# Blockwise causal attention and a gated unit on one core: q and k loaded nine tokens to a partition, two pairs on the two halves, under a new written order

## The chip, the core and the metric

The kernel runs on one NeuronCore of a Trainium2 chip. TensorE (PE in the profile, its weight loads PEld) multiplies matrices, VectorE (DVE), ScalarE (ACT) and GpSimd (POOL) work elementwise, and SyncE (SP) issues nearly all transfers, which 16 DMA engines carry out. The metric is the time of one execution on the device in microseconds (us), lower is better. Three runs of the kernel before took 183.25, 184.25 and 185.91 us, a median of 184.25 us.

## The reference: what is computed

q, k and v have 8 batches, 8 heads, 576 tokens and 64 channels in float32. A query attends to every key of its own block of 64 tokens and of the blocks ahead of it. The heads' outputs stand beside each other as x (576 x 512 for each batch), which a gated unit takes on.

```python
scores = (1 / sqrt(64)) * q @ k.transpose(0, 1, 3, 2)
mask = block_i >= block_j                 # block = position // 64
attn = softmax(where(mask, scores, -1e9))
x = heads side by side of (attn @ v)
gate = sigmoid(sum over 5 taps of conv_w[t] * x shifted by t - 4 tokens)
out = (gate * (x @ w_val)) @ w_out
```

## The kernel before

**Units of work.** Two heads of a batch are a pair, numbered p = 0 to 31, four pairs to a batch. For its attention each pair sees 512 tokens in blocks of 128, and the last 64 tokens of a batch's eight heads, the tail, go a way of their own. Heads h = 0 and 1 of a pair lie on partitions 0 to 63 and 64 to 127 once transposed, so that two matmuls with 64 rows stand side by side in the array.

**Steps of a pair.** `lq` and `lk` (line 258) load 512 tokens of the two heads, four tokens to a partition on all 128 partitions, so that a run in memory is four tokens or 1 KB, 256 KB in all, into one of five buffers `qks`. `lv` (line 274) loads v for one head, in runs of 256 B. `cq` casts q and k of a pair to fp16 in one instruction of 128 x 1024, mostly on POOL (line 246), `cv` casts v. `T` transposes the pair with 16 transposes on PE (line 141), and `Te` copies the result from PSUM to `qkT` with the tokens back in order, 128 x 1024, on DVE (line 246) or ACT (line 244). `S` makes the scores in three pieces of 512 columns for each head (line 137), and `E` is their exponential, 128 x 1024, always on ACT (line 458), 96 in all. `mka` and `mkb` zero on POOL what the block mask cuts out of them (lines 481, 483, 487). `A` multiplies with v and a column of ones, `N` normalizes on DVE (lines 508, 509), `X` transposes and `Xe` copies into the ring `xt` of the unit's input.

**The tail.** `lt` (line 281) loads the last 64 tokens of q or k of all eight heads of a batch in two transfers with runs of 512 B, `ct` casts them on POOL, `TT` transposes them with an identity sorted by head (`byhead`), `TTe` copies them to `ktails`. The third score piece of a pair multiplies four key blocks with the tail's 64 queries, one matmul of 64 columns for each block and head. `lvt` (line 288) loads v's tail on 64 partitions, 128 KB. `SL` and `EL` are the tail's scores with itself, `AT`, `NT`, `XT` and `XTe` its attention.

**The unit.** For each of ten runs of 464 columns of `xt`, `C` is the convolution (80 matmuls of 32 x 32), `CS` its tanh on ACT (line 617), `V` the product with w_val, and `Ve` multiplies the two on DVE (line 635). `O` multiplies 128 tokens with w_out, `Oe` copies to `osb`, and `Od` (line 660) writes 256 KB out from SP.

**What sets the order.** `PLAN` is a list of words, such as `S/1.0/P/6+7`, in the order in which the program is written: step, arguments, engine, PSUM banks. Each engine works through its own words in that order and waits by semaphores where data or a buffer is not there yet. SP is one such queue: a load whose buffer is not free yet, or an `Od` whose rows are not ready yet, holds all transfers behind it.

Of the kernel before, what the change touches and what calls it, by code (L numbers as in the profile page):

```python
# [12 lines left out]
lk/1/S ppool//G pdve//V lcv//S ccv//G CW//P/1 lq/1/A cq/1/V T/1/P/4+5 lq/0/S lk/0/S lt/0.1/S  # L13
lt/0.0/S ct/0/G lk/4/S lq/3/S CWe//V lk/3/S cq/3/G cq0/0/V T0/0/P/0+1 lq/2/S lk/2/S lq/4/S cq0/1/V
T0/1/P/2+3 Te/1/A pact//A S/1.1/P/4+5 lv/1.0/S lv/0.0/S lv/0.1/S S/1.0/P/6+7 lt/1.0/S lq/5/S
lv/2.1/S T0e/0/V lk/5/S T0e/1/A S/0.0/P/2+3 lv/1.1/S lv/2.0/S lvt/0/S lv/3.1/S lt/1.1/S TT/0/P/0+1
lk/6/S TTe/0/V lv/3.0/S lq/6/S cq/4/G E/1.1/A E/0.0/A lwv/1/S lwv/0/S SL/0/P/0+1 EL/0/A S/0.2/P/2+3
E/1.0/A S/1.2/P/4+5 E/1.2/A S/0.1/P/0+1 T/3/P/6+7 cq/2/V T/2/P/4+5 mka/1/G cv/0/G Te/3/A S/3.1/P/6+7
E/0.1/A T/4/P/0+1 Te/2/V S/2.2/P/4+5 lwo/1/S lwo/0/S E/0.2/A mka/0/G mkb/0/G lk/7/S S/2.1/P/2+3
lq/7/S lt/2.0/S Te/4/V S/4.0/P/0+1 E/3.1/A E/2.2/A E/2.1/A S/2.0/P/6+7 E/2.0/A A/0/P/4+5 S/3.2/P/6+7  # L20
cq/5/V T/5/P/2+3 lt/2.1/S lk/8/S lv/4.1/S lq/10/S E/4.0/A N/0/V cv/2/V X/0/P/4+5 mkb/1/G cv/1/G
A/1/P/0+1 lq/8/S Xe/0/V E/3.2/A S/4.1/P/4+5 N/1/V S/3.0/P/6+7 mkb/3/G mkb/2/G mka/2/G Te/5/A
S/5.0/P/2+3 lk/10/S E/4.1/A ct/1/G cv/3/G lv/4.0/S A/2/P/0+1 N/2/V lq/9/S lk/9/S lv/6.0/S E/3.0/A
mka/3/G S/5.1/P/4+5 E/5.1/A TT/1/P/6+7 TTe/1/V lv/5.1/S cvt/0/G cq/6/G A/3/P/0+1 N/3/V cwv/1/G
cwo/0/G E/5.0/A ct/2/G lv/7.1/S S/4.2/P/6+7 SL/1/P/4+5 lv/6.1/S EL/1/A mka/4/G cq/7/G E/4.2/A
mkb/4/G cq/8/G lq/13/S lv/5.0/S lv/7.0/S lvt/1/S lk/12/S lq/12/S lk/11/S lq/11/S AT/0/P/2 X/1/P/4+5
X/3/P/0+1 Xe/3/A T/6/P/6+7 Te/6/A X/2/P/0+1 Xe/2/A NT/0/V XT/0/P/3 S/6.0/P/6+7 E/6.0/A Xe/1/V
C/0/P/0+1+4+5 CS/0.1/A CS/0.0/A XTe/0/V cwv/0/V V/0.3/P/7 cwo/1/V Ve/0.3/V V/0.0/P/6 Ve/0.0/V
S/6.1/P/4+5 E/6.1/A W//P/0+1+2+3 We/0/A We/1/V S/5.2/P/6+7 TT/2/P/4+5 TTe/2/V V/0.2/P/2 SL/2/P/0+1
S/6.2/P/4+5 E/5.2/A T/7/P/6+7 Ve/0.2/V Te/7/V EL/2/A E/6.2/A V/0.1/P/0 S/7.0/P/4+5 E/7.0/A mka/5/G  # L30
T/8/P/6+7 S/7.1/P/2+3 E/7.1/A Ve/0.1/V cv/4/G A/4/P/0+1 Te/8/V S/8.2/P/6+7 N/4/V E/8.2/A O/0.2/P/4
Oe/0.2/A mkb/5/G S/8.1/P/0+1 E/8.1/A X/4/P/2+3 mka/6/G cq/10/G Xe/4/V cq/9/G T/9/P/6+7 T/10/P/6+7
Te/9/V S/8.0/P/4+5 E/8.0/A O/0.0/P/2 Oe/0.0/V S/7.2/P/0+1 E/7.2/A S/9.2/P/4+5 E/9.2/A cv/6/G mkb/8/G
Te/10/V mkb/6/G A/6/P/2+3 cv/5/G A/5/P/0+1 N/6/V mka/7/G S/9.0/P/6+7 S/9.1/P/4+5 E/9.0/A mkb/7/G
cv/7/G A/7/P/2+3 lk/13/S E/9.1/A lt/3.0/S N/5/V X/5/P/2+3 S/10.1/P/6+7 E/10.1/A lq/14/S lt/3.1/S
cvt/1/G AT/1/P/0 S/10.0/P/4+5 E/10.0/A O/0.1/P/1 Oe/0.1/A lk/14/S N/7/V Xe/5/V NT/1/V XT/1/P/0
X/6/P/6+7 Xe/6/A XTe/1/V X/7/P/2+3 cq/12/G T/12/P/4+5 cq/11/G T/11/P/4+5 lv/9.1/S S/10.2/P/0+1
E/10.2/A cq/13/G mka/9/G Xe/7/V C/1/P/2+3+6+7 lv/8.1/S CS/1.0/A ct/3/G cq/14/G mka/8/G Te/11/V
Te/12/V lv/8.0/S lq/15/S cv/8/G mkb/9/G V/1.0/P/1 Ve/1.0/V V/1.1/P/0 Ve/1.1/V CS/1.1/A lk/15/S
lv/9.0/S lt/4.1/S S/11.1/P/2+3 lvt/2/S lv/11.1/S lt/4.0/S E/11.1/A lv/11.0/S lk/17/S T/13/P/4+5  # L40
TT/3/P/4+5 lq/17/S lv/10.0/S lv/10.1/S lq/18/S lk/18/S Te/13/V S/11.0/P/6+7 E/11.0/A V/1.3/P/1
Ve/1.3/V T/14/P/2+3 Te/14/V mkb/10/G cv/9/G lv/12.0/S mka/11/G S/11.2/P/6+7 V/1.2/P/0 TTe/3/A
E/11.2/A S/13.1/P/4+5 mkb/11/G lv/12.1/S Ve/1.2/V S/14.1/P/2+3 S/13.2/P/6+7 cq/15/G A/8/P/0+1
E/13.1/A O/0.4/P/4 ct/4/G E/13.2/A S/13.0/P/6+7 N/8/V E/14.1/A lq/16/S lk/16/S Oe/0.4/V A/9/P/0+1
S/12.0/P/2+3 X/8/P/4+5 E/13.0/A T/15/P/4+5 N/9/V S/12.1/P/6+7 S/12.2/P/0+1 E/12.0/A E/12.1/A
lv/13.1/S Te/15/V Xe/8/V X/9/P/2+3 E/12.2/A cv/11/G A/11/P/2+3 N/11/V O/0.5/P/7 lt/6.1/S Oe/0.5/A
Xe/9/V S/14.0/P/5+6 mka/10/G cvt/2/G lv/13.0/S cq/17/G TT/4/P/0+1 T/17/P/0+1 X/11/P/0+1 Te/17/V
mka/12/G E/14.0/A S/14.2/P/2+3 cv/10/G cq/18/G AT/2/P/7 E/14.2/A O/0.3/P/6 Oe/0.3/A TTe/4/V Xe/11/V
T/18/P/4+5 Te/18/A S/17.0/P/2+3 E/17.0/A lv/14.1/S lv/14.0/S A/10/P/0+1 NT/2/V cv/12/G mkb/12/G
mkb/13/G A/12/P/6+7 S/17.1/P/4+5 E/17.1/A mka/13/G N/10/V w0/1.64.0/P/0 S/18.1/P/0+1 E/18.1/A  # L50
X/10/P/2+3 N/12/V Xe/10/V lk/19/S cq/16/G T/16/P/6+7 Te/16/V S/15.0/P/4+5 E/15.0/A lv/15.0/S
lv/15.1/S cv/13/G A/13/P/2+3 SL/3/P/0+1 EL/3/A cv/14/G lk/20/S lvt/3/S lq/19/S S/18.0/P/6+7 E/18.0/A
S/16.2/P/4+5 mkb/14/G E/16.2/A Od/0.0/S mka/14/G N/13/V mka/18/G mka/17/G C/2/P/0+1+2+3 CS/2.1/A
# [59 lines left out]
def kernel(  # L113
# [10 lines left out]
    nc = tc.nc  # L124
# [310 lines left out]
    def S(p, t, eng, bank):  # L435
# [3 lines left out]
        s = both(bank)  # L439
# [302 lines left out]
```

## Time and profile before

| | |
|---|---|
| median of three runs | 184.25 us (183.25 to 185.91) |
| span of the profiled execution, first to last instruction | 180.0 us |
| what lies around the span, by the median | 4.25 us |
| PE busy | 159.7 us, 89% |
| ACT busy | 137.3 us, 76% |
| DVE busy | 122.6 us, 68% |
| POOL busy | 82.6 us, 46% |
| read from memory, written | 30.42 MB, 9.44 MB |
| share of the DMA engines taken by SP's and ACT's queues | 76.0% and 0.9% |
| granted TensorE clock | 1.000 |

The page tells of the profiled execution only its span; the time around it is taken as the difference to the median of the runs. Busy shares are averages over the whole span, and the stages differ: the transfers in come first, the exponentials last till about four fifths, and what follows is the unit's matmuls. Matmuls overlap, so a PE that is shown busy is not full. "<-" in a group names what is read, and after "idle before" it names what ended the engine's waiting.

### The profile page before, as it was taken

Reading aid. Unit: us, or ns where it says so; the run is one execution under the profiler, and the core shown is the slowest. Engines: PE = TensorE matmul, PEld = TensorE weight load, DVE = VectorE, ACT = ScalarE, POOL = GpSimd, SP = SyncE. Lnnn points to the kernel's source line nnn. Section 1 sums busy time; section 2 is a strip of 40 time slices with the busy share of each in tenths; the row PEclk is TensorE's granted clock in tenths of the full one; section 3 lists DMA queues with packets and bytes.
Section 4 is the critical chain, followed back from the end, with each engine's and each line's share of the span. In section 5 each row is a group of like instructions: output and inputs, shape, how many; then the busy total and the mean of one; then the engine's idle time right before and its main releaser. Section 6 shows DMA issues by size and latency. Waiting matters only on the chain.

```text
span 180.0 us, 8228 instructions
## 1 busy us (share of the span) xinstructions
PE 159.7 (89%) x3513; PEld 98.5 (55%) x3513; DVE 122.6 (68%) x249; ACT 137.3 (76%) x162; POOL 82.6 (46%) x198
## 2 busy tenths in 40 slices
PE   0567987779989998899899999999999999999991
PEld 0343765345754665656555755566775557455450
DVE  6635665687869786669748896587984876935640
ACT  2499999889979997989798989988996753333432
POOL 6326372677674677547467437462930622000000
PEclk9999999999999999999999999999999999999999
DMA  5899899997978799969999997998796006063366
GB/s 171 255 302 228 195 326 358 267 271 171 292 223 233 175 281 243 236 200 269 296 214 273 329 275 193 293 284 224 229 319 167 0 4 230 6 232 127 117 235 232
DMA packets 66494, 40.39 MB, mean 224 GB/s; under 512 B 40213, under 2 KB 60949, under 8 KB 66458
## 3 DMA queue, kind: packets, MB, share of 16 engines
q1 hardware_dynamic: 65898, 39.35, 76.0%
q8 instruction: 27, 0.44, 1.1%
q10 hardware_dynamic: 560, 0.52, 0.9%
q14 instruction: 9, 0.07, 0.1%
HBM read 30.42 MB, written 9.44 MB: 221 GB/s over the span
## 4 chain that ended last, share of the span: by engine, by line
PE 59%; DMA 14%; SPq 9%; ACT 6%; issue 4%; DVE 3%; POOL 2%; POOLq 0%; DVEq 0%
PE PS L137 54%; PE PS L141 5%; DMA qks<-in_q_dram 5%; ACT pt L458 4%; SPq L258 4%; DMA qks<-in_k_dram 3%; DMA vs<-in_v_dram 3%; SPq L281 3%; SPq L274 2%; DMA conv_nat<-in_moe_conv_w_dram 2%; DMA vts<-in_v_dram 2%; ACT qkT L244 1%; DVE x L509 1%; DVE qkT L246 1%; POOL qk L246 1%
## 5 line engine op out<-in xcount | busy, mean ns | idle before, releaser
L458 ACT ACTIVATE pt<-PS 128x1024 f16<-128x1024 f32 x96 | 93.1, 1041 | 10.6 <-PE PS L137 9.0
L246 POOL CAST qk<-qks 128x1024 f16<-128x1024 f32 x28 | 29.0, 1041 | 18.8 <-DMA qks<-in_k_dram 9.1
L137 PE MATMUL PS<-xt,w_val 128*128 128x464 f16 x160 | 36.5, 360 | 0.5 <-DVE w_out L600 0.3
L137 PE MATMUL PS<-qkT 64*128 64x256 f16 (+3 forms) x256 | 34.0, 319 | 3.0 <-DVE qkT L246 1.2
L137 PE MATMUL PS<-w_out,gv 128*128 128x512 f16 (+1 forms) x148 | 35.6, 374 | 0.0
L635 DVE SCALAR_TENSOR_TENSOR gv<-th,PS 128x112 f16<-128x112 f32 (+4 forms) x64 | 26.1, 449 | 10.2 <-ACT th L617 5.1
L137 PEld LDWEIGHTS <-pt 128*128 128x128 f16 (+1 forms) x960 | 28.0, 103 | 8.0 <-issue 4.0
L137 PE MATMUL PS<-v,pt 128*128 128x65 f16 (+1 forms) x896 | 31.4, 196 | 0.8 <-POOL v L246 0.3
L246 DVE COPY qkT<-PS 128x1024 f16<-128x1024 f16 (+1 forms) x24 | 28.7, 1199 | 4.7 <-PE PS L141 3.0
L137 PEld LDWEIGHTS <-qkT 64*128 64x128 f16 x512 | 17.5, 98 | 16.6 <-issue 9.4
L617 ACT ACTIVATE th<-PS 128x928 f32<-128x928 f32 x20 | 17.8, 947 | 9.9 <-PE PS L137 9.5
L246 POOL CAST v<-vs 128x512 f16<-128x512 f32 x31 | 19.2, 622 | 12.0 <-DMA vs<-in_v_dram 8.7
L509 DVE TENSOR_TENSOR x<-PS,rc 128x512 f16<-128x512 f32 x32 | 22.1, 692 | 1.1
L137 PEld LDWEIGHTS <-w_val 128*128 128x128 f16 x160 | 13.9, 98 | 14.1 <-issue 2.6
L137 PEld LDWEIGHTS <-gv 128*128 128x128 f16 x148 | 13.0, 98 | 13.3 <-issue 1.5
L246 DVE COPY osb<-PS 128x512 f32<-128x512 f32 x18 | 12.4, 690 | 7.6 <-PE PS L137 5.2
L141 PE MATMUL PS<-ident,qk 64*128 64x64 f16 x512 | 13.8, 199 | 3.9 <-POOL qk L246 1.3
L246 DVE COPY xt<-PS 128x512 f16<-128x512 f16 (+1 forms) x34 | 13.1, 399 | 5.4 <-PE PS L141 3.2
L481 POOL MEMSET pt<- 64x256 f16 x32 | 9.8, 306 | 14.0 <-ACT pt L458 13.0
L244 ACT COPY osb<-PS 128x512 f32<-128x512 f32 x17 | 10.0, 586 | 7.0 <-PE PS L137 4.5
L141 PEld LDWEIGHTS <-qk 64*128 64x128 f16 x512 | 11.1, 100 | 7.2 <-POOL qk L246 2.8
L508 DVE RECIPROCAL rc<-PS 128x8 f32<-128x8 f32 x32 | 6.6, 205 | 12.2 <-PE PS L137 9.6
(62 smaller groups left out, 134.3 us busy)
## 6 DMA issues: line engine op xcount, KB each, us to landing
out_dram<-osb SPq DMA_DIRECT2D x35, 256.0 KB, 3.3
qks<-in_k_dram SPq DMA_DIRECT2D x32, 256.0 KB, 4.7
vs<-in_v_dram SPq DMA_DIRECT2D x64, 128.0 KB, 4.3
qks<-in_q_dram SPq DMA_DIRECT2D x31, 256.0 KB, 4.6
tls<-in_k_dram SPq DMA_DIRECT2D x16, 64.0 KB, 4.1
tls<-in_q_dram SPq DMA_DIRECT2D x16, 64.0 KB, 3.6
vts<-in_v_dram SPq DMA_DIRECT2D x8, 128.0 KB, 4.0
gv<-in_moe_w_val_dram SPq DMA_DIRECT2D x2, 512.0 KB, 6.9
```

Source lines behind the costliest of these rows:

```text
L137: made.append(nc.tensor.matmul(out=out, lhsT=lhsT, rhs=rhs, start=start, stop=stop, skip_group_check=True))
L141: made.append(nc.tensor.transpose(out=out, in_=in_, identity=identity))
L244: i = nc.scalar.copy(out=out, in_=in_)
L246: i = (nc.vector if eng == "V" else nc.gpsimd).tensor_copy(out=out, in_=in_)
L258: DMA[eng].dma_start(out=rot(qks, p)[0:128, i], in_=(q, k)[i][b, 2 * g:2 * g + 2, 0:512, 0:64].rearrange("h (p n) d -> p h (n d)", n=4))
L281: DMA[eng].dma_start(out=tls[b % 2][0:128, i, r], in_=(q, k)[i][b, 0:8, 512:576, 0:64].rearrange("(g r) (p n) d -> r p g (n d)", r=2, n=2)[r])
L458: made.append(nc.scalar.activation(out=rot(pts, p)[0:128, 0:2, 512 * t:512 * t + 512], in_=both(take("S", p, t)), func=AF.Exp, bias=0.0, s ...
L481: nc.gpsimd.memset(pt[64:128, 0:2, 0:1024].rearrange("p h (t s) -> p h t s", t=2)[:, :, :, 0:64], 0.0)
L508: made.append(nc.vector.reciprocal(out=rc[0:128], in_=r[:, :, :, 64:65]))
L509: made.append(nc.vector.tensor_tensor(out=rot(x16, p)[0:128].rearrange("p i h d -> p h i d"), in0=r[:, :, :, 0:64], in1=rc[0:128].to_broad ...
L617: made.append(nc.scalar.activation(out=rot(ths, n)[0:128, 2 * i:2 * i + 2], in_=both(take("C", n, i))[:, :, 0:RUN], func=AF.Tanh, bias=0.0 ...
L635: made.append(nc.vector.scalar_tensor_tensor(out=gv[0:128, x, a - 4 * i:e - 4 * i], in0=rot(ths, n)[0:128, x, a - o:e - o], scalar=1.0, in ...
```

## The change

A load of q or k now takes all 576 tokens of the pair's two heads, nine tokens to a partition, on 64 partitions: an even pair on partitions 0 to 63, an odd pair on 64 to 127. A run in memory is nine tokens or 2304 B, and a load is 288 KB. Two pairs, u = 0 to 15, share a buffer, and there are three buffers for q and three for k. One cast `cd` (128 x 1152) takes q or k of two pairs, one `Tt` transposes them with 18 transposes, one `Te` (128 x 1152) puts them in order. The first two pairs are cast and transposed by themselves (`cp`, `Tp`, `Tep`). The tail's loads, casts, transposes and copies are gone (`lt`, `ct`, `TT`, `TTe`, `byhead`, `ktails`): the tail's queries are columns 512 to 575 of the same `qkT`, and columns 576 to 639 of the keys are zeroed once. The third score piece of a pair is now one matmul of 320 columns and three of 64 for each head, where it was one of 256 and four of 64. `mka` and `mkb` zero the same cells in one instruction each. One warming matmul (`w0`) is gone.

The written order is new as a whole. Against the old one it moves 13 of the 32 casts of v from POOL to DVE (one was there), two of the eight of v's tail, three of 30 casts of q and k; ACT has 6 of 30 `Te` (8 of 31 before), 21 of 35 `Oe` (17), 6 of 32 `Xe` (3), two of the four first casts and four issues of loads (one before).

```diff
-    qks = consts(5, [128, 2, 2, 256], fp32, "qks")
+    qks = [consts(3, [128, 2, 576], fp32, f"{n}s") for n in "qk"]
...
     def load_qk(i, p, eng):
         b, g = divmod(p, 4)
+        u, x = divmod(p, 2)
         DMA[eng].dma_start(
-            out=rot(qks, p)[0:128, i],
-            in_=(q, k)[i][b, 2 * g:2 * g + 2, 0:512, 0:64].rearrange(
-                "h (p n) d -> p h (n d)", n=4))
+            out=rot(qks[i], u)[64 * x:64 * x + 64],
+            in_=(q, k)[i][b, 2 * g:2 * g + 2, 0:576, 0:64].rearrange(
+                "h (p n) d -> p h (n d)", n=9))
...
+    def cast(i, u, hs, eng):
+        copy(eng, rot(qk16[i], u)[hs].rearrange("p n h d -> p h n d"),
+             rot(qks[i], u)[hs].rearrange("p h (n d) -> p h n d", n=9))
+
+    @op
+    def cd(u, i, eng, bank=None):
+        cast(i, u, slice(0, 128), eng)
...
+    @op
+    def Tt(u, i, eng, bank):
+        o = place(bank, TRIPLES, "Tt", u, i)
+        for n in range(9):
+            halves(both16(bank), o + 64 * n, rot(qk16[i], u)[0:128, n])
+
+    @op
+    def Te(u, i, eng, bank=None):
+        bank, o = placed("Tt", u, i)
+        copy(eng, rot(qkT, u)[0:128, i, 0:2, 0:576].rearrange("p x (s n) -> p x s n", n=9),
+             both16(bank)[:, :, o:o + 576].rearrange("p x (n s) -> p x s n", n=9))
...
     def S(p, t, eng, bank):
...
-            work = [(0, 2, 256, 512)] + [(256 + 64 * j, j, None, None) for j in range(4)]
+        work = ([(0, 0, 0, 512)], [(0, 3, 384, 512), (128, 1, 128, 512)],
+                [(0, 2, 256, 576), (320, 0, 512, 576), (384, 1, 512, 576), (448, 3, 512, 576)])[t]
```

More of the change, by code (lines that the diff above doesn't have):

```diff
@@ L312, in pdve, with pd1 @@
         nc.vector.tensor_copy(out=ident16[0:128], in_=ident[0:128])
[L313 to L314 removed]
+    @op
+    def pd1(eng, bank=None):
         for i in range(4):
@@ L425, in TTe @@
[L425 to L431 removed]
+            where["Tp", p, i] = bank[i]
+            for n in range(9):
+                turn(out=one16(bank[i])[:, 64 * n:64 * n + 64], in_=rot(qk16[i], u)[hs, n],
+                     identity=ident16[hs, hs])
```

324 lines of the change are left out of this document (131 added, 193 removed).

## The prediction

> **What bounds the kernel now.** I read the busy shares in 40 slices first, then the windows, then the chain, then the transfers.
>
> ```profile
> PE   0567987779989998899899999999999999999991
> ACT  2499999889979997989798989988996753333432
> DMA  5899899997978799969999997998796006063366
> ```
>
> Each digit is 4.5 us. The DMA engines are full from the second slice to about 137 us, ACT till about 140 us, PE from about 90 us to the end. So there are two stages, and the windows price them (columns: PE, PEld, DVE, ACT, POOL busy, clock, DMA share, GB/s):
>
> ```profile
> 10.00:20.00 10.00, 7.46 (x124) 4.80 (x126) 4.66 (x7) 9.71 (x12) 4.65 (x10) 1.00 0.99 250
> 20.00:40.00 20.00, 16.57 (x426) 11.06 (x422) 13.59 (x24) 18.12 (x22) 11.09 (x24) 1.00 0.98 296
> 40.00:60.00 20.00, 18.43 (x460) 11.63 (x457) 16.13 (x30) 17.81 (x21) 12.22 (x24) 1.00 0.80 221
> 60.00:80.00 20.00, 18.38 (x471) 12.34 (x469) 13.85 (x29) 18.44 (x22) 13.93 (x34) 1.00 0.90 239
> 100.00:120.00 20.00, 20.00 (x468) 12.29 (x467) 14.88 (x28) 18.19 (x21) 10.57 (x24) 1.00 0.99 272
> ```
>
> From 10 to 80 us PE idles 9.2 us and ACT 5.9 of 70, while DMA is taken for 0.80 to 0.99. From 100 on PE has no idle time left. The chain that ended last agrees: ahead of 70 us it runs over transfers and SP's issues, from 89 us over PE alone.
>
> ```profile
> 24.50 8.35 DMA qks<-in_q_dram
> 62.98 5.08 DMA qks<-in_k_dram
> 154.54 21.78 PE PS L137 x256
> ```
>
> (start, us, what.) Two loads of 256 KB hold the chain for 8.35 and 5.08 us. Time lost in the first stage isn't got back, since PE is full in the second. The last exponential ends at 147.2, PE at 176.3; 3.7 us of copy and write follow.
>
> **Base: the change if transfers bind as little as now.** On PE the transposes stay 576 (512 of pairs and 64 of tails before; 32 x 18 after). The third score piece has one 64-column matmul less for each pair and head; on full PE (89 to 176 us) these start 21.5 ns apart on the mean. Of the 43 ns of the two heads, 27 come back as the columns of the longer matmul (two of 512, side by side, start 213 ns after the next two: 0.42 ns a column): 16 ns x 32 = 0.5 us gained.
>
> ACT's words up to the last exponential, by the rows' means: 96 E at 1.041 = 99.9 in both. Before besides: 14 CS at 0.947, 9 Oe at 0.586, 8 Te at 1.027, 8 EL at 0.600, 3 Xe, 2 TTe, 2 XTe, We and small ones, 37.5 in all: 137.4. After: 16 CS, 13 Oe, 6 Te at 1.14 (1.027 drawn out to 1152 elements), 8 EL, 6 Xe, two first casts at 1.14, two Tep and small ones, 44.0: 143.9, 6.5 more. Before, 138.5 us from the first to the last exponential held 137.4; at that pace the last exponential ends 6.6 us later, at 153.8. In return PE's words behind it are fewer: 8 V instead of 11 (4 x 196 ns each), 10 O instead of 14 (4 x 216 ns), one C (1.2) and some small ones less, 20.1 us instead of 28.1, and 28.1 took 29.1 before, so 20.8. 153.8 + 20.8 + 3.7 = 178.3. That is 1.7 below the span, and PE's stream by itself gives 0.5 below. **Base: 179 us of span.**
>
> What else moves lies under cover. POOL loses 12 us: casts of q, k and tails 34.1 become 33.9, 12 casts of v at 0.622 go to DVE (7.5), the masks go from 96 memsets (0.306, 0.199, 0.199) to 64 (at 0.306 each, 3 us less). It stood idle for over half of the span. DVE's row sum goes from 126 to 129 in a span of 180, with 32% idle. SP issues 32 transfers less; at 0.5 to 0.65 us each that frees 16 to 21 us of an engine that waits anyway. The start: before, q and k of the first pair had landed by 4.5 us and the first exponential began at 8.71. After, two loads (0.74 to 5 us), cast on POOL and ACT side by side (1.041 x 1152/1024 = 1.17), 18 transposes (at 19 to 29 ns, 0.5), two copies side by side (0.7), scores (0.5): 8.5, even, or 1 later where the loads are slower. If ACT's four issues (0.48 each) weren't covered by the loads in flight, 1.4 more.
>
> **The loads decide.** Bytes hardly change: 64 loads of 288 KB for 64 of 256 KB and 32 of 64 KB. But each now goes to 64 partitions. Where the queue was backed up (an issue over 2.2 us ahead of the landing before it), I took the times between landings from the trace: a load of q or k of 256 KB lands 0.74 us after the one ahead by the median, 0.81 on the mean; of v (128 KB, 128 partitions) 0.44 and 0.51; an output 0.67 and 0.88; weights 1.58. The only load on 64 partitions is the tail of v:
>
> ```profile
> vs<-in_v_dram SPq DMA_DIRECT2D x64, 128.0 KB, 4.3
> vts<-in_v_dram SPq DMA_DIRECT2D x8, 128.0 KB, 4.0
> ```
>
> Issue to landing tells nothing here, as it holds the queue. But where a vts followed a vs at once, it landed 0.93, 0.78, 0.49 and 0.80 us behind, 0.75 on the mean: 1.48 times the 0.51 of the same bytes in the same 256 B runs on twice the partitions. It's thin (around 91.5 us packets slowed from 18 to 30 ns, which they also did at 39 us without a vts), and the other four are mixed with other loads. Bounds for a load of 288 KB: below 0.91 (0.81 x 9/8, by bytes), above 1.69 (0.75 x 288/128). I take the ratio on the nearest size: 0.91 x 1.48 = **1.35 us**.
>
> Sum of the queue in the written order, from about 3 us on. Up to the q of pair 10: 24 x 1.35 + 16 v x 0.51 + 2 x 0.75 + 4 x 1.58 = 48.4, landing at 51.4; cast 1.17, transposes 0.3, copy 1.36 (1.221 x 1152/1024), scores 0.3 later its first exponential could start, at 54.5. By ACT's words it is due at 48.3: up to the 32nd exponential they sum to 44.7 in both orders, which ended at 50.4 before, and this is the 31st. Late by 6. Up to the k of pair 30: 64 x 1.35 + 62 x 0.51 + 8 x 0.75 + 4 x 1.58 + 16 outputs x 0.88 = 144.5, at 147.5; with 3.1 for the chain and 8 for the exponentials and tanhs still to come, the last ends at 158.6 instead of 153.8, late by 5. This holds with no gap in the queue. Before, the same sum to the load that landed at 40.2 us gives 36.5, so 3.7 us were gaps; and now SP waits for three buffers of two pairs, where a load goes out only once the cast from the same buffer, three units back, is done, and an output that waits for late rows holds loads behind it. Without gaps +6, with gaps of that size +9.7: I take +7. 179 + 7 = 186 of span, and 4.25 around it: **190 us**.
>
> Beside this stands the Trainium skill, SBUF — State Buffer, section Door 1: transfers to 64 partitions in one half reach 8 of 16 ports, and it measured 196 GB/s against 328 at 1 MiB. By 196 GB/s a load is 1.50 us, the sum to pair 30 is 154, and the time would be about 197. Its next section finds only 6% gained from two transfers on the two halves, which speaks against this change, as the loads of the two pairs would then not run beside each other. No run here shows that rate; the four landings point the same way.
>
> **Rivals.**
>
> *Loads as cheap as their bytes (0.91 us).* Runs of 2304 B instead of 1 KB and 512 B speak for it, and most packets of vts took the same 18 ns as those of vs. Then pair 10 is there at 44.4, pair 30 in time by 20 us, and the base stays: 179 + 4.25 = 183. The point from which loads decide is 1.1 us: (48.3 - 6.1 - 16) / 24, where 6.1 is the start and the chain, 16 the other loads.
>
> *The other side: the gaps of the first stage close.* With loads at 0.91, 32 issues less on SP, three units of buffers (six pairs for five) and POOL 12 us lighter, the waits that kept POOL's casts back (9.1 and 6.2 us on k and q, 8.7 on v) go, and PE's 9.2 us of idle time from 10 to 80 us shrinks by 7: 172 of span, 176. It needs loads under 1.1 us. Against it: ACT idles only 5.9 there and has 6.5 us more to do.
>
> *Loads at the upper bound, 1.69.* The sum to pair 30 is 166, landing at 169, the last exponential at 180, the end at 204.5 of span, 209 with what lies around. Halves one after the other in one queue, and v's runs no faster, would do it.
>
> *The change doesn't do what it says:* if the two loads of a unit ran beside each other on the halves, it is the first rival.
>
> **Numbers.** Forecast 0.50 (own range 184 to 197), loads by bytes 0.20 (180 to 186), gaps closed 0.15 (172 to 180), upper bound 0.15 (197 to 209). The range leaves out the lower half of the third and the upper half of the fourth: 176 to 202. A measurement here tells about 2% from no change (180.6 to 187.9): faster 0.17; same 0.28 (the second rival and a fifth of the forecast's); slower 0.55.
>
> **What would show it.** Right: GB/s between 10 and 60 us at or under the 221 to 296 of before with the DMA engines as full, packets of 2304 B well over 9/4 of the 46 ns that 1 KB took in the median; waits of POOL's casts on q and k over the 15.3 us of before (9.1 + 6.2); the chain on loads of q and k far past 63 us; PE idle over 9.2 us from 10 to 80. PE's 64-column group at 192 instead of 256 and the same pace in the second stage would show the base. Wrong: loads landing 0.9 us apart, or ACT's words spread in a way that its sum to the last exponential doesn't tell; a cast or copy of 1152 elements with nine-fold stride much over 1.17 or 1.36 would add 0.2 us x 30 on POOL or DVE, under cover unless the loads are late.

## The result and the profile after

The change made the kernel slower. The median went from 184.35 us (183.25 to 185.91, four runs) to 208.77 us (207.69 to 211.83, four runs), 1.141 times as long with a 95% interval of 1.126 to 1.156. The forecast was 190, with a range up to 202. The profiled execution took 208.98 us with a span of 207.2, so 1.8 us lay around the span.

First the busy shares in 40 slices of the kernel after, 5.2 us each, with the clock that TensorE was granted:

```profile
PE   0466639996778787969982899999998999999992
ACT  2389274895777666856982578898798997947243
PEclk9999985999996999978999699999999999999999
DMA  5999999699999999999999999989599962024065
```

The DMA engines are now full, but for two slices, from the second slice to about 165 us; before, it was 137. PE, which before stood at 8 or 9 from the tenth slice on, has a 2 at 109 us, and its clock falls four times, which it didn't before. The windows of the kernel after have the same columns as those of before (PE, PEld, DVE, ACT, POOL busy, clock, DMA share, GB/s):

```profile
10.00:20.00 10.00, 6.78 (x120) 4.73 (x116) 5.53 (x9) 8.65 (x10) 5.49 (x14) 1.00 1.19 228
20.00:40.00 20.00, 13.61 (x316) 9.84 (x316) 10.76 (x20) 11.27 (x14) 8.01 (x14) 0.83 1.02 230
40.00:60.00 20.00, 15.76 (x328) 9.11 (x326) 14.26 (x26) 15.25 (x18) 9.65 (x15) 1.00 1.10 189
60.00:80.00 20.00, 15.20 (x349) 9.69 (x347) 12.06 (x23) 13.43 (x16) 9.46 (x17) 0.91 1.17 185
100.00:120.00 20.00, 14.52 (x353) 8.28 (x350) 9.12 (x20) 11.99 (x15) 5.22 (x10) 0.91 1.05 221
```

Fewer bytes a second move although the engines are busy throughout: 185 to 230 GB/s where it was 221 to 296. (A share over 1 means that the packets' recorded times overlap.) PE idles 18.7 us between 10 and 80 us, where it was 9.2. The chain holds long transfers up to 88 us, and ends on PE (start, us, what):

```profile
2.75 9.69 DMA ks<-in_k_dram
20.38 9.95 DMA vs<-in_v_dram
42.50 7.57 DMA vs<-in_v_dram
50.09 8.45 DMA qs<-in_q_dram
67.29 9.07 DMA vs<-in_v_dram
81.96 6.09 DMA vs<-in_v_dram
...
190.16 11.63 PE PS L135 x56
```

Of these six transfers, four are loads of v, which the change doesn't touch. The loss is complete well ahead of the end. The end of the 16th, 32nd, 64th and 96th exponential and the span, in us:

| | 16th | 32nd | 64th | 96th | span |
|---|---|---|---|---|---|
| before | 26.2 | 50.4 | 100.0 | 147.2 | 180.0 |
| after | 37.7 | 65.5 | 129.3 | 184.0 | 207.2 |
| after, q and k on all partitions (first experiment) | 33.2 | 57.9 | 109.6 | 164.8 | 188.0 |

From the 64th exponential on, the kernel after and the version with cheap loads go at the same pace (54.7 and 55.2 us). Between them everything is lost before 130 us: 4.5 us up to the 16th exponential, 3.0 up to the 32nd and 12.1 from there to the 64th.

### The profile page after: what moved, and what is told of

Same layout as the page of the kernel before. It is cut to its first block, busy times and chain, and to the rows that moved or that the text cites. A ratio compares the mean times of both kernels' runs of the same rounds, so it can differ in the third digit from the quotient of the medians.

```text
span 207.2 us, 8007 instructions
## 1 busy us (share of the span) xinstructions
PE 167.5 (81%) x3448; PEld 102.2 (49%) x3448; DVE 124.4 (60%) x246; ACT 143.0 (69%) x170; POOL 74.8 (36%) x145
## 3 DMA queue, kind: packets, MB, share of 16 engines
q1 hardware_dynamic: 52938, 38.56, 87.2%
## 4 chain that ended last, share of the span: by engine, by line
PE 48%; DMA 25%; SPq 9%; DVE 5%; issue 5%; ACT 4%; POOL 2%; ACTq 0%; POOLq 0%; DVEq 0%
PE PS L135 44%; DMA vs<-in_v_dram 16%; DMA ks<-in_k_dram 5%; DMA qs<-in_q_dram 4%; PE PS L139 4%; SPq L253 4%; SPq L269 4%; DVE x L469 2%; ACT qkT L238 2%; POOL v L240 1%; ACT pt L416 1%; DVE xt L240 1%; SPq L280 1%; DVE rc L468 1%; DVE qkT L240 1%
## 5 line engine op out<-in xcount | busy, mean ns | idle before, releaser
L135 PE MATMUL PS<-v,pt 128*128 128x65 f16 (+1 forms) x896 | 34.8, 202 | 10.7 <-POOL v L240 3.2
L135 PE MATMUL PS<-qkT 64*128 64x64 f16 (+4 forms) x512 | 39.0, 262 | 3.9 <-DVE qkT L240 2.9
L240 DVE COPY qkT<-PS 128x1152 f16<-128x1152 f16 (+1 forms) x26 | 33.9, 1308 | 13.3 <-PE PS L139 13.2
L595 DVE SCALAR_TENSOR_TENSOR gv<-th,PS 128x112 f16<-128x112 f32 (+5 forms) x64 | 26.0, 447 | 20.1 <-PE PS L135 11.1
L240 POOL CAST k<-ks 128x1152 f16<-128x1152 f32 (+1 forms) x15 | 17.2, 1147 | 20.8 <-DMA ks<-in_k_dram 16.2
L240 POOL CAST q<-qs 128x1152 f16<-128x1152 f32 (+1 forms) x14 | 16.2, 1161 | 15.6 <-DMA qs<-in_q_dram 11.0
L444 POOL MEMSET pt<- 64x256 f16 x32 | 10.4, 329 | 28.0 <-ACT pt L416 26.7
L135 PE MATMUL PS<-xt,DG 32*32 32x464 f16 x800 | 14.4, 391 | 7.4 <-issue 4.8
L238 ACT COPY osb<-PS 128x512 f32<-128x512 f32 x21 | 12.3, 587 | 10.8 <-PE PS L135 10.4
L439 POOL MEMSET pt<- 64x256 f16 x32 | 10.1, 316 | 26.4 <-ACT pt L416 24.2
L240 POOL CAST v<-vs 128x512 f16<-128x512 f32 x19 | 12.3, 649 | 15.0 <-DMA vs<-in_v_dram 14.4
L139 PE MATMUL PS<-ident,q 64*128 64x64 f16 x288 | 8.2, 196 | 11.1 <-ACT q L238 7.6
```

The lines of the kernel that those rows point to most:

```text
L135: made.append(nc.tensor.matmul(out=out, lhsT=lhsT, rhs=rhs, start=start, stop=stop, skip_group_check=True))
L139: made.append(nc.tensor.transpose(out=out, in_=in_, identity=identity))
L238: i = nc.scalar.copy(out=out, in_=in_)
L240: i = (nc.vector if eng == "V" else nc.gpsimd).tensor_copy(out=out, in_=in_)
L439: nc.gpsimd.memset(rot(pts, p)[64:128, 0:2, 0:1024].rearrange("p h (t s) -> p h t s", t=2)[:, :, :, 0:64], 0.0)
L444: nc.gpsimd.memset(rot(pts, p)[64:128, 0:2, 640:1408].rearrange("p h (t s) -> p h t s", t=2)[:, :, :, 0:64], 0.0)
```

## The experiments

All ratios are to the kernel before, run on the same chip beside them.

### q and k on all 128 partitions

The edit undoes one thing, the half of the partitions. The bytes, the 2304 B runs, the buffers and the written order stay.

```diff
-            out=rot(qks[i], u)[64 * x:64 * x + 64],
+            out=rot(qks[i], u)[0:128, x],
...
-                "h (p n) d -> p h (n d)", n=9))
+                "h (p n) d -> (h p) (n d)", n=9))
```

> The changed kernel with one thing altered: each load of 288 KB goes to all 128 partitions (one run of 2304 B a partition, the two heads on the two halves, a pair's load in one half of the free dimension) instead of to 64 partitions with two runs. Bytes, runs, number of loads, written order and every other instruction stay; the heads stand in the wrong places, so the scores are of mixed heads, and the first two pairs wait for one load more each. Theory (the half of the partitions makes the load slow, and v's loads with it): the 2304 B packets fall from 169 to about 105 ns, v's 256 B packets from 27 to under 20 ns, the time to 180-187 us. Rival one (the written order, the coarser units and the longer instructions are at fault): packets change, the time stays above 200. Rival two (runs of 2304 B are slow by themselves): packets stay near 169 ns and the time above 200.

Measured: 189.73 us, a ratio of 1.041 (1.032 to 1.051), a little over the 187 us that the theory allowed. The transfers' queue in the kernel after, and then in this one (queue, packets, MB, share of 16 engines' span):

```profile
q1 hardware_dynamic: 52938, 38.56, 87.2%
```

```profile
q1 hardware_dynamic: 52938, 38.56, 72.0%
```

These are the same packets and the same bytes. The half of the partitions alone turns 72.0% of 188.0 us (135 us) into 87.2% of 207.2 us (181 us). A packet of 2304 B takes 93 ns by the median on all partitions and 167 on the halves. So the halves cost about 19 us here. The other 4% stay.

### The kernel before with its loads on the halves

The same test from the other side: the written order, the tail and the runs of before, only q on partitions 0 to 63 and k on 64 to 127, eight tokens a partition. A run grows from 1 to 2 KB with it, and the casts read the new places.

```diff
-    qks = consts(5, [128, 2, 2, 256], fp32, "qks")
+    qks = consts(5, [128, 2, 512], fp32, "qks")
...
-            out=rot(qks, p)[0:128, i],
+            out=rot(qks, p)[64 * i:64 * i + 64],
...
-                "h (p n) d -> p h (n d)", n=4))
+                "h (p n) d -> p h (n d)", n=8))
...
```

> The kernel before with one thing altered: q of a pair is loaded to partitions 0 to 63 and k to 64 to 127, eight tokens or 2 KB a run, instead of four tokens or 1 KB a run on all 128. Bytes, number of loads, casts and order stay; tokens and q and k stand in the wrong places. Theory (half the partitions): 2 KB packets of loads near 150 ns instead of the 84 that 2 KB take elsewhere, a load about 1.2 us instead of 0.74 behind the one ahead, v's loads slower too; 64 x 0.46 = 29 us more queue time and some 15 for v, of which the slack of the queue (about 180 - 137 us) takes part: 193-206 us. Rivals (order, runs): longer runs are cheaper or equal, 181-186 us.

Measured: 201.95 us, a ratio of 1.108 (1.101 to 1.116). The halves cost about a tenth under either order: 1.108 here, and 1.141 over 1.041, or 1.096, there.

### The transfers by themselves

The kernel holds loads in groups of one kind, each group of q and k waiting for the one before (all arithmetic is left out). Some loads of v ran ahead beside the other groups, so the times below are taken between landings of one kind.

```python
full:  out=big[0:128, j // 2, j % 2]                # 288 KB on 128 partitions
half:  out=big[64 * x:64 * x + 64, j]               # 288 KB on 64; x alternating or 0
v:     out=vb[0:128, j]                             # 128 KB, runs of 256 B
vhalf: out=vb[0:64, 2 * j:2 * j + 2]                # 128 KB on 64 partitions
```

> Transfers alone, no attention and no unit (only the first 128 rows of the output are written, with zeros): eight phases, each waiting for the one ahead. 1: 16 loads of 288 KB on 128 partitions. 2: 16 on alternating halves. 3: 16 all on the lower half. 4: as 2, the upper half issued from ACT. 5: 16 loads of v (128 KB, 256 B runs). 6: 8 loads of v's tail (128 KB on 64 partitions). 7: phases 1 and 5 mixed one to one. 8: phases 2 and 5 mixed one to one. Theory (halves are slow, also in turn): per load 0.83 us in 1, 1.35 in 2, 3 and 4, 0.45 in 5, 0.6-0.75 in 6, 1.3 a couple in 7, 1.8-2.1 in 8, where more than 1.8 shows v slowed by its neighbours. If the two halves run beside each other: 0.83-0.9 in 2 and 4 and 1.35 in 3 alone. If only the runs matter: 1, 2, 3 and 4 are equal.

Measured, as the mean time from one landing to the next:

| group | us a load |
|---|---|
| 288 KB on 128 partitions | 0.75 |
| 288 KB, halves in turn, one queue | 1.26 |
| 288 KB, lower half only | 1.45 |
| 288 KB, halves in turn, issued by SP and ACT in turn | 1.09 |
| v, 128 KB on 128 partitions | 0.60 |
| v's tail, 128 KB on 64 partitions | 0.77 |
| a full load and a v in turn, both together | 1.34 |
| a half load and a v in turn, both together | 2.02 |

The windows of the same run show the rates (columns here: DVE busy, POOL busy, clock, DMA share, GB/s; the rows are the first four groups, v's tail and the two couples):

```profile
27.20:36.20 9.00, 0.00 (x0) 0.00 (x0) 1.00 1.07 372
43.80:58.90 15.10, 0.00 (x0) 0.00 (x0) 1.00 1.06 231
64.60:84.90 20.30, 0.00 (x0) 0.00 (x0) 1.00 1.05 206
93.20:107.30 14.10, 0.00 (x0) 0.00 (x0) 1.00 1.09 273
115.70:120.30 4.60, 0.00 (x0) 0.00 (x0) 1.00 0.96 202
128.50:139.30 10.80, 0.00 (x0) 0.00 (x0) 1.00 1.10 317
145.10:175.50 30.40, 0.00 (x0) 0.00 (x0) 1.00 1.12 206
```

The DMA engines are full or nearly so in each row, and the rate goes with the partitions. The rows hold some packets of other groups, the fifth 162 packets of full loads above all: by its landings v's tail moved at 170 GB/s (128 KB in 0.77 us). The reader is to see the last row. A couple of a half load and a v moves at 206 GB/s, though v goes to all partitions; by themselves the two take 1.26 and 0.60 us, together they take 2.02. Of the 0.68 us that the couple of halves takes longer (2.02 against 1.34), 0.51 are the half load's own (1.26 against 0.75), and 0.17 come on top where the two are mixed.

The Trainium skill, SBUF — State Buffer, section Door 1, gives 196 GB/s at 1 MiB for 64 partitions of one half and 328 for all. The rows agree: 206 against 372, at 288 KB. The Trainium skill also gives, on the same page in section "Can I just issue two DMAs to hit both halves?", 6% gained by two transfers on the two halves. Here the halves in turn gain 12% in rate (231 against 206), and 32% when two engines issue them (273).

### What the order costs without late loads

Two kernels leave out all loads of q and k but the first six (after) or five (before) pairs'; the casts read old data again.

```diff
     def load_qk(i, p, eng):
+        if p >= 6:
+            return
```

> The changed kernel, but q and k are loaded for the first three units (pairs 0 to 5) alone; every later cast reads again what lies in the buffers, so the outputs of the later pairs are computed from q and k of earlier ones. Casts, transposes, scores and the written order stay. It asks what the new order costs when the loads of q and k can't be late. Theory one (what was left of the loss with cheap loads, 189.7 us, lies in the order, the units of two pairs and the start): the time stays at 187 to 191. Theory two (what was left lies in the transfers, in gaps that the buffers make): it falls to the base, 179 of span and 1.8 around it, 181, or lower.

> The kernel before, but q and k are loaded for the first five pairs alone (tails, v, weights and outputs as they were); later casts read again what lies in the buffers, so later pairs are computed from q and k of earlier ones. It gives the other base, to be set against the same of the changed kernel. If transfers held the kernel before by PE's idle time from 10 to 80 us, up to 9 us go: 174 to 179. If that idle time was the order's own, 0 to 3 us go: 180 to 184. The difference to the changed kernel without its loads is what the order is worth by itself: I had taken it at 179 against 180 of span, that is nothing; with theory one of the run beside it, it is 6 us or more.

Measured: the kernel after without them 190.91 us (1.036, 1.027 to 1.044), the kernel before without them 179.80 us (0.977, 0.971 to 0.983). The new order is no faster than with cheap loads (190.91 against 189.73), though SP's queue falls to 47.1% of the engines; the old one gains 4.3 us. With no load of q or k to come late from the seventh pair on, the new order is 11 us slower than the old one. Of these, 9 are there at the 16th exponential (35.6 us against 26.6). The first units' loads, still on the halves, can be at most a part of that: with all loads on all partitions it ends at 33.2. The first line is the kernel after, the second the kernel before, each without those loads (busy time and share of the span, instructions):

```profile
PE 163.2 (86%) x3448; PEld 100.3 (53%) x3448; DVE 123.2 (65%) x246; ACT 142.3 (75%) x170; POOL 74.8 (39%) x145
```

```profile
PE 158.4 (89%) x3513; PEld 97.6 (55%) x3513; DVE 123.1 (69%) x249; ACT 137.1 (77%) x162; POOL 83.0 (47%) x198
```

From the 16th to the 96th exponential PE is busy 123.4 of 130.7 us after and 113.8 of 118.2 us before, ACT 112.0 and 106.2. So in this stage PE is nearer to its limit than ACT in both, and it has 9.6 us more to do there in the new order.

### v left out

The kernel after on the halves, with v loaded for the first five pairs alone.

```diff
     def lv(p, h, eng="S", bank=None):
+        if p >= 5:
+            return
```

> The changed kernel with q and k on the halves as they are, but v is loaded for the first five pairs alone (its last 64 tokens still for every batch); later casts of v read again what lies in the buffers, so the outputs are those of other v. Theory one (the loss on top of 189.7 us is the queue's sum, 64 loads on halves and 62 of v between them): without 52 loads of v at 0.87 us the sum to pair 30 is 64 x 1.35 + 10 x 0.87 + 6 + 6.3 + 14 = 121, nowhere late, and the time falls to 186 to 191. Theory two (half loads bind by themselves, or stalls of PE and the lower clock cost the time, not the queue): it stays at 200 or over.

Measured: 198.42 us, a ratio of 1.076 (1.067 to 1.086). That is 10 us less than the kernel after, and 7.5 more than with q's and k's loads left out; neither theory's number came. The trace explains a part. (The profile is of the execution that took 203.6 us, so only its places are read here, not its sums.) The chain has a step of 4.26 us in which nothing was waited for:

```profile
40.88 0.34 PE PS L139 x16
41.22 4.26 issue
45.48 0.24 PE PS L139 x2
```

PE stops in the middle of 18 transposes that all need the same cast, 16 done and two to go. The cast had ended at 40.56 us.

### PE's pauses without a wait

The kernel after has such a pause too, 4.84 us long. Counting all that the trace has of PE's queue (matmuls, weight loads and a dozen that only wait) in order of start, the first instruction behind a pause of over 0.35 us is 1985, 2241 and 3521 in that kernel, and with few v 705, 961, 1473, 3521 and 4289. All are 193 over a multiple of 256. (The expectations count up to the first matmul, and say 195.) The instruction queue moves one packet of 16 KB for each 256 instructions of PE, and each pause ended 1.3 to 2.0 us after such a packet had ended. So it looked as if PE waited for its next block of instructions. Three kernels tested this, one of them the kernel after once more, the others with 128 instructions put ahead of PE's stream (the line of `PLAN` is shown in part):

```diff
+    def sh(n, eng, bank):
+        for _ in range(n):
+            mm(one(bank)[:, 0:64], ident16[0:128, 0:128], ident16[0:128, 0:64])
...
-pdve//V px//G
+pdve//V sh/64/P/3 px//G
```

> The changed kernel as it is, profiled once more. PE's pauses that no wait explains stood at PE's instructions 1987, 2243 and 3523 (matmuls and weight loads counted together), which are 256 x 7, 8 and 13 plus 195. Theory one (PE waits there for its next block of 256 instructions, a packet of 16 KB that stands behind the loads on the DMA engines): pauses again at counts of 195 over a multiple of 256 and nowhere else, not always at the same ones, each ending 1.3 to 1.7 us after a packet of the instruction queue, and the clock at half right behind pauses of over 1.5 us. Theory two (a chance event or a wait that the profile doesn't name): none, or at other counts. Time 207 to 212.

> The changed kernel with 64 matmuls of 64 columns on a free PSUM bank written first on PE, which add 128 instructions (64 matmuls, 64 weight loads) ahead of all others, in time that PE has free before the first transpose. Theory one (blocks of 256 instructions): the pauses keep to counts of 195 over a multiple of 256 in the new stream, that is to other words of the kernel, 128 instructions earlier than before. Theory two (the pause belongs to the word, its banks or its data): they stay with the words, at counts of 195 + 128 over a multiple of 256. Time 205 to 213 by both.

> The changed kernel with v loaded for the first five pairs alone, and the same 64 matmuls ahead of PE's stream. Without them its pauses stood at counts 707, 963 (4.26 us), 1475, 3523 and 4291 (1.77 us), all 195 over a multiple of 256. Theory one: pauses over 0.35 us at 195 over a multiple of 256 again, so at other words; what they cost together, 7.5 us there, may be anything from 1 to 8, and the time follows it: 192 to 200. Theory two: they stay with the words, 128 counts later, and the time stays at 198.

Measured: 210.62, 212.98 and 203.13 us, with 184.97 for the kernel before beside them. The pauses:

| kernel | at instruction | together |
|---|---|---|
| before | 3521 | 0.4 us |
| all partitions | 961, 2753 | 1.8 us |
| after | 1985, 2241, 3521 | 7.2 us |
| after again | 1985, 2241, 3009, 3521 | 6.8 us |
| after, shifted by 128 | 961, 1729, 1985, 3777, 4289, 4545, 5825, 6849 | 14.8 us |
| few v, shifted by 128 | 961, 1729, 3777, 4289, 6849 | 9.4 us |

Every one is 193 over a multiple of 256, and so are all 53 such pauses in the 17 traces of whole kernels here. (At 1729, 1.72 and 1.94 us, the profile names a copy on DVE that had ended 0.6 and 0.8 us before PE went on, so a part of these two is a wait for it.) The places keep to the count and not to the words. By theory two the shifted kernels would pause at a remainder of 65. In both executions the kernel after paused at the same instruction of the same run of the convolution; shifted by 128 it doesn't pause there but in other groups. The first two are the kernel after and the same once more, the third the shifted one (PE's instructions in order of time; in brackets the idle time and what ended it):

```profile
108.64 1.18 PE L135 MATMUL PS<-xt,DG 32*32 32x464 f16 x51
114.66 1.57 PE L135 MATMUL PS<-xt,DG 32*32 32x464 f16 x62 [4.84 <-issue]
```

```profile
108.76 1.30 PE L135 MATMUL PS<-xt,DG 32*32 32x464 f16 x66
114.85 1.73 PE L135 MATMUL PS<-xt,DG 32*32 32x464 f16 x52 [4.79 <-issue]
```

```profile
34.28 0.85 PE L135 MATMUL PS<-xt,DG 32*32 32x464 f16 x44
39.05 1.34 PE L135 MATMUL PS<-xt,DG 32*32 32x464 f16 x36 [3.92 <-issue]
```

Theory one holds. In the kernel after, PE crossed into the block that ended at 109.83 at 106.9 us, the packet of the next block started 4.9 us later, at 111.8, and had ended at 113.2; PE went on at 114.66. In the kernel before, packets started 0 to 3.4 us after the crossing, and PE hardly ever waited. The Trainium skill, Runtime: NRT & Kernel Launch, section Instruction fetch mechanics, says that instructions come in blocks of 16 KiB, 256 each, by transfers that the sequencer starts itself, which the places agree with. It calls the cost mostly hidden, which holds for the kernel before (0.4 us) and not here (7.2).

### What is left with cheap loads

Four kernels ask where the 4% of the first experiment come from. The first splits DVE's long copies in one for each pair, the second mends the start of the order, both with the first experiment's loads (lines of `PLAN` are shown in part here):

```diff
-    copy(eng, rot(qkT, u)[0:128, i, 0:2, 0:576].rearrange("p x (s n) -> p x s n", n=9),
+    for x in range(2):
+        copy(eng, rot(qkT, u)[0:128, i, x, 0:576].rearrange("p (s n) -> p s n", n=9),
...
```

```diff
-cp/1.0/A pt//G lk/4/S cp/0.0/G ccv//V
+cp/1.0/A lk/4/S cp/0.1/G cp/0.0/G pt//G ccv//V
...
-cp/0.1/A pd1//V S/1.0/P/0+1 S/1.2/P/4+5 CWe//V E/1.2/A
+S/1.0/P/0+1 S/1.2/P/4+5 E/1.2/A
...
-Tep/0.0/A lv/1.1/S
+Tep/0.0/A pd1//V CWe//V lv/1.1/S
```

> The changed kernel with q and k on all partitions (189.7 us, 1.041 times before), and each of DVE's long copies of turned q or k (1152 elements a partition, two pairs, 1.31 us) as two, one for each pair, so that the scores of a unit's first pair can start after the first half. Theory one (what is left of the loss comes from units of two pairs: PE waits for copies that are twice what it needs next): 1 to 3 us less, 187 to 189. Theory two (it lies in the start and in words of PE that stand further apart): no change or up to 1 us more, since the two copies take 0.2 us more together.

> The changed kernel with q and k on all partitions, and the start of the written order mended: the cast of the second k leaves ACT, where it stood ahead of the first exponential, for POOL ahead of the memsets; DVE's four copies of the folded identity and the product behind it come after the first pair's copies. The first exponential, at 11.28 us with this order and at 8.71 before, should start at about 10. If the start were what is left of the loss, 2.5 to 3 us of 7.4 would go with as much of the start; I expect 0.5 to 1.5 less, 188 to 189, since PE's idle time to 10 us is only 1.5 us over that of before.

Measured: 191.31 and 190.14 us. (The runs of before beside them spread from 179.7 to 185.9, so the ratios of 1.060 and 1.055 say less than the times.) Neither helps. The first exponential of the second still began at 11.28 us: with every load on all partitions, a first cast, which reads one half of them, had to wait for the loads of both pairs. The k of pair 1 had landed at 4.6 us and its cast began at 7.62. That wait came from the experiment, not from the change, so two more kernels load the first unit on the halves and the rest on all partitions, the first with the start mended and the second with the order of the change:

```diff
-            out=rot(qks[i], u)[0:128, x],
+            out=rot(qks[i], u)[64 * x:64 * x + 64] if u == 0 else rot(qks[i], u)[0:128, x],
...
```

> The changed kernel with the loads of q and k on all partitions from the second unit on, the first unit (pairs 0 and 1) on the halves as in the change, and the start of the written order mended as in the run before (cast of the second k on POOL, folded identity later). With all loads on all partitions the first cast, which reads one half of the partitions, waited for the loads of both pairs: the k of pair 1 had landed at 4.7 us and its cast began at 7.62. If that wait of 2.9 us is what is left of the loss, the first exponential starts at about 8.5 to 9 and the time falls by 2 to 3 us, to 187; if PE's words set the time from then on, it falls by 1 or less.

> The same loads (first unit on the halves, all others on all partitions), with the written order of the change as it is, so that the cast of pair 0's k stands ahead of the first exponential on ACT. Against the run beside it, it prices that place in the order: the first exponential then starts behind the landing of pair 0's k, at 10 to 11 us, and the time is 0 to 1.5 us longer than beside it. By theory two (the start is made good later, since PE's stream is what binds) both are within 1 us of 189.7.

Measured: 192.38 us (1.041, 1.032 to 1.049) with the start mended, 189.66 us (1.024, 1.017 to 1.032) without. The first exponential began at 10.75 and 12.27 us, and the kernel whose exponentials begin sooner is the slower one: its 16th ends at 36.3 us, the other's at 32.0. So neither the place of that cast nor the first exponential's time explains what is left. With loads that are cheap after the first unit the new order costs 2.4 to 4.1%. In the second of the two, PE's busy time is as before (159.5 us against 159.7), and the whole loss is PE's idle time, 28.0 us against 20.3: 1.5 more up to 10 us, 2.4 more at block borders, 1.3 at 22.9 us for a cast of v, the rest in waits of at most 1.1 us each.

### TensorE's clock

The page shows a full clock up to 29 us in the kernel after, but its first record of the clock is at 26.2 us, and at 21.3 in the kernel before. What PE does ahead of that shows half the clock. These are two groups of 20 matmuls of the same kind in the kernel before, ahead of the first record and behind it (start, us):

```profile
18.20 1.28 PE L137 MATMUL PS<-v,pt 128*128 128x65 f16 x20
...
22.99 0.77 PE L137 MATMUL PS<-v,pt 128*128 128x65 f16 x20
```

Single matmuls of 65 columns start 54 ns apart there and 29 later, in every version at its own first record. So, by this pace, each kernel begins at half clock and comes to full clock at 21.3 us before, 26.2 after, and 29.5 with all loads on all partitions. In the kernel after, the clock also falls to half for 6.8 us from 29.6 and for 3.4 us each from 63.8, 91.1 and 115.0. In the 3.4 us ahead of these, PE had been busy for 1.55, 1.97, 1.53 and 0.29 us; the last is the long pause. PE's busy time follows the time at half clock: 159.7 us with 21.3, 162.6 with 29.5, 167.5 with 43.2 in the kernel after. To see whether this costs time, matmuls on zeros were added where PE waits in the first stage:

```diff
+    def sh(n, eng, bank):
+        for _ in range(n):
+            mm(one(bank)[:, 0:512], wz[0:128, 0:128], wz[0:128, 0:512])
...
-pdve//V px//G
+pdve//V sh/18/P/0 px//G
...
```

> The kernel with the first unit's loads on the halves and all others on all partitions (189.66 us), with 39 matmuls of 512 columns on zeros added in seven places of PE's stream up to the scores of pair 3, where PE waits, so that PE is busy from 1.5 us on. In all traces matmuls of 65 columns start 54 ns apart until the first record of the clock (21.3 us before, 26.2 after, 19.6 to 35.2 in the others) and 29 ns from there, so TensorE runs at half its clock until then. Theory one (the new order loses part of its time because PE comes to full clock late and at half clock takes twice as long for its words): full clock from 6 to 10 us on, PE's own words shorter by 2 to 4 us, the time 186 to 188.5. Theory two (loads and ACT set the first stage, the clock doesn't matter there): 189 to 191.

> The kernel before, with 23 such matmuls in six places up to the transposes of pair 3. Theory one: full clock from 6 to 10 us on instead of 21.3, a gain of 1 to 3 us, 181 to 183. Theory two: 184 to 185. If theory one holds this beats both kernels.

> The changed kernel with the same 39 matmuls as the first of these. PE's half clock lasted 26.2 us at the start and 17 us later on. Theory one: the first falls to 6 to 10 us, those behind 29 us stay, since they follow waits for loads: 205 to 208. Theory two (loads decide): 208 to 210.

Measured: 191.49, 184.92 and 210.12 us, ratios of 1.052 (1.037 to 1.066), 1.017 (1.006 to 1.029) and 1.153 (1.139 to 1.167). (The runs of before beside them spread from 180.8 to 185.7, so the ratios say less than the times; one more execution of the first took 386.27 us, which nothing here explains.) The full clock came at 6.1, 5.5 and 3.9 us, fell again for some windows, and no kernel got faster. Theory two's numbers came, within 0.5 us. But the added matmuls have a price of their own: in the kernel before, the 16th exponential ends at 28.2 us with them and at 26.2 without. So a gain of that size from the clock may be hidden, and what is shown is only that this way of getting the full clock earlier is worth nothing. The later falls weren't tried.

## Why the prediction was wrong

**What held.** The half load's price was taken at 1.35 us. It lands 1.26 us after the one before by itself in turn, and 1.34 on the mean in the kernel after (k 1.46, q 1.22, where SP issued the two transfers one after the other well ahead); 169 ns of a packet's time x 128 packets / 16 engines is 1.35. The number was in part luck: a full load by itself takes 0.75 us and not 0.91, and the halves cost 1.68 times that and not 1.48, the ratio of v's tail (0.77 to 0.60 is only 1.28). The threshold of 1.1 us was passed, packets of 2304 B took more than 9/4 of the 46 ns, and the waits of POOL's casts on q and k went from 15.3 to 27.2 us. What lies behind the last exponential takes 23.2 us; the prediction had 20.8 and 3.7, or 24.5. The rivals with loads by bytes and with closed gaps are refuted by 1.26 us, over the 1.1 that both need. The rival at the upper bound named 209 us, which came, but by luck: its load of 1.69 us doesn't occur, and too much for a half load made up for too little for a v.

**Where the 21 us of span are that the forecast lacked.** It had 186 of span, the kernel 207.2. Going from the version with cheap loads to the kernel after, PE's busy time grows from 162.6 to 167.5 and its idle time from 25.3 to 39.7:

| step of the prediction | predicted, us | measured, us |
|---|---|---|
| base (cheap loads), span | 179 | 188.0 |
| late loads: PE's idle time over the base, without pauses | +7 | +9.0 (14.4 less 5.4) |
| PE's pauses at blocks of 256 instructions, over the base | not foreseen | +5.4 (7.2 less 1.8) |
| PE's busy time, with 43 us at half clock instead of 29.5 | not foreseen | +4.9 (167.5 less 162.6) |
| span | 186 | 207.2 (0.1 lost in rounding) |
| around the span | 4.25 | 1.8 |

These are parts of PE's time in two traces. The last three together are the 19.2 us of span that the halves cost, where the prediction had 7. The split is of PE's time and not of causes. Late loads leave PE idle, which goes along with its lower clock, and PE's instructions come late when the DMA engines are busy with half loads, but no run took one of these away by itself. Nor do they simply add up: the second execution of the kernel after reached the 64th exponential at 129.2 us too, with 10.2 us of later half clock instead of 17.0, and the shifted kernel, with 9.5 us of pauses up to there, at 123.4. Of the kernel's three pauses only the longest, 4.84 us, stands in the chain that ended last.

**The base: the step that failed first.** It was 179 us and is 188.0 with cheap loads. Two terms were wrong. The first is the start, "8.5, even, or 1 later": against the kernel before, 5.8 to 10.1 us are lost up to the 16th exponential with cheap loads (7.0 in the first experiment), and the first exponential begins at 10.8 to 12.3 us there and at 12.1 in the kernel after (11.0 in its second execution). The second is the pace. "At that pace the last exponential ends 6.6 us later" took ACT's words as the pace up to the last exponential. PE was nearer to its limit: with few loads of q and k, PE is busy for 0.94 of the time between the 16th and the last exponential in the new order and for 0.96 in the old. The new order has eight us less of V, O and C behind the last exponential, and the prediction took them off there; but PE then has them to do ahead of it. From the 64th to the 96th exponential the versions with cheap loads and the kernel after need 54.7 to 55.3 us (the second execution of the kernel after 56.4), the old order 47.3, and that takes back nearly 8 of the 9.6 us that are gained behind the last exponential (32.8 to 23.2). From the 16th exponential to the end the first experiment is thus only 1.0 us longer than before; most of its 8.0 us are lost ahead of that. "PE's stream by itself gives 0.5 below" was the right bound to use, but not with the idle time of before: with cheap loads PE stood idle for 25.3 us instead of 20.3 and was busy for 162.6 instead of 159.7. (The 0.5 us of that bound isn't there either: on full PE the two heads' matmuls of 64 columns start 28 to 29 ns after the two before, not 43.) It stays open which of the order's words do this: a mended start, split copies and an earlier full clock gave nothing back, and a whole other order wasn't tried.

**The lateness: the step that failed most.** "I take +7" for late loads; the halves cost 19.2 us of span. The half load's own price was right. "Of v 0.44 and 0.51" was kept from before. In the kernel after a v lands 0.87 us after the transfer ahead on the mean (0.60 with cheap loads), and the couple of a half load and a v, summed at 1.86, takes 2.02 by itself. The queue's sum was short by that: 62 x 0.36 is 22 us, and the k of pair 30 landed at 166.5 us, not at 147.5. Up to the 32nd exponential the forecast was near: it had the 31st late by 6, and the 32nd is 7.5 us later than with cheap loads. The rest was to be no more ("late by 5" at the last one), but 12.1 us are lost between the 32nd and the 64th. PE is idle there for 11.0 of 63.8 us instead of 3.6 of 51.7 (7.2 of the 11.0 in its three pauses) and busy for 4.7 us more, with 8.5 us at half clock. From the 64th on the pace is that of the cheap loads, so the late last loads didn't hold the end, though the prediction had them do so. What was late by the chain came for the most part from v's loads (four of its six long transfers), which the prediction treated as others' cost. Leaving most loads of v out took 10 us away, leaving those of q and k out 18 of the 19: the half loads are the cause, and v's loads in the same queue are a part of how they act. (Two sums of the first rival are a little off, 43.9 for its 44.4 us and 23 for its 20, which changes nothing.)

**The gaps and what lies around.** The +1 for gaps in SP's queue can't be told apart in these runs. The 4.25 us around the span were the difference of a profiled span to a median of other runs; the profiled execution of the kernel after has 1.8, and the other runs here have 1.7 to 2.0.

## What to carry to other kernels

A load that goes to 64 partitions moved at 206 to 231 GB/s here against 372 on 128, with the same runs, and it slowed the transfers mixed with it; price a change of layout by the partitions that a load touches before its run length. When words are moved from the tail to the middle of a program, charge them to the engine that has no idle time there, even if another engine seems to give the pace. And a queue of slow loads can have a second price, which a sum of transfers doesn't show: PE's own instructions came late here, and its clock fell where it had been idle.

## What the runs showed of the hardware that was not expected

- PE's instructions arrive in blocks of 256, and with q and k on the halves PE stood still for up to 4.84 us at their borders (0.37 in the kernel before), at the same instruction in two executions and at shifted words when 128 instructions were put ahead. PE went on 1.3 to 2.0 us after the block's packet had ended.
- TensorE ran at half its clock for the first 20 to 35 us of the kernels without added matmuls, though the page shows it as full for want of a record, and again for 3.4 or 6.8 us behind windows of 3.4 us in which PE had been busy for 0 to 2 us. The Trainium skill, TensorE: Matmul & The Clock Gate, section The HAM clock gate, tells of a cold start at half clock, of such a window and of half the clock after an idle one; here windows that were busy for up to 1.97 of 3.4 us had the same effect, and matmuls that bring the full clock earlier were worth nothing.
- v's packets of 256 B, on all partitions, took 24 ns by the median between half loads and 18 without.
- Halves issued by two engines in turn moved 273 GB/s, by one 231, on the lower half alone 206.
